# The order of weight loads, statistics and splits beside the experts' blocks of a routed layer, and which experts run in f32

## The chip, the cores and the metric

One Trainium2 chip, one core. The metric is the device time of one execution, in microseconds; of several runs the median is given.

## What is computed

```python
def reference(q, k, v, ...):
    x = attention(q, k, v)                  # causal by blocks of 64; 4 x 8 heads, 576 tokens, 64 wide
    x = x.transpose(0, 2, 1, 3).reshape(2304, 512)
    h = x @ w_in                            # 512 -> 2048
    x = elu(h) @ w_out                      # 2048 -> 512
    do = x @ w_skip > 0                     # about half of the tokens go on
    e = argmax(x[do] @ w_gate); gate = softmax's largest
    out = x.copy()
    for each expert i of 8:                 # w1[i] 512 x 1024, w2[i] 1024 x 512
        m = do & (e == i)
        out[m] += gate[m] * (relu(x[m] @ w1[i]) @ w2[i])
    return out
```

All inputs and the output are f32. With these inputs 1216 tokens are routed: 176, 2, 5, 91, 283, 192, 453 and 14 to the experts 0 to 7.

## The kernel before, in words

Attention and the dense layer run in chunks of 256 tokens, the last two stages of a chunk beside the next one's first; each chunk's tokens are routed as soon as it is through. After the last routing the experts follow. Expert 0's first 128 tokens and expert 2's (64 places) are known earlier and run beside the last routing. Then come **sections**: expert 6, 4, 5 (`ORDER`; 2 has nothing left), and a last section that holds the first block of each expert in `LAST`, 0, 3, 1 and 7. A section's first block is issued by `first_tokens`, further blocks of 128 tokens by `more_tokens` inside branches on the expert's count. First blocks of the experts in `SMALL` have 64 tokens. So with these inputs section 6 has four blocks of 128, section 4 has 64, 128 and 128 tokens, section 5 has 64 and 128, and the last one 64 tokens for 0, 1 and 7 and 128 for expert 3.

Tokens of a block are gathered by GpSimd (`gp`), transposed by SyncE's DMA (`mxt`, `mxwo`), multiplied with `w1` on TensorE (`hp`), made `r` and `hh` by ScalarE (`relu`) and VectorE, multiplied with `w2` (`y`), scaled by ScalarE into `o` and added to the output by GpSimd. In the last section experts of `PLAIN`, 1 and 7, are multiplied in f32, where one product is compiled into two instructions of TensorE; all others with f16 halves, three products for one.

For f16 the weights have to be prepared. An expert's weights are eight pages of 512 KB: half 0 is `w1` (four pages), half 1 is `w2`. A half is **loaded** by SyncE (`load_w`, L1447 and L1450), then come **statistics** of each page (`stat_w`, ScalarE L1465 into `jk` or VectorE L1467), a **scale** (`scale_w`: small steps on VectorE and one matmul `ns`, as TensorE sums over partitions) and **splits** of each page into high and low halves (`split_p`, ScalarE L1495 and VectorE L1496). A page needs a place in a list `FREE`, which is that of a page split before; the transfer waits until it is read.

What is prepared beside which block is written in the string `PREP`: section, colon, then a part per block between bars. `l` is a load, `s` the statistics, `c` the scale, `p` the splits; `c4-1` is expert 4, half 1. `split_beside` records these steps, `tokens` the block's. `Recorder.order` puts all steps of a part in an order by estimated costs, steps of the block (`urgent`) ahead and others where they fit in before the next urgent step of the engine; `rc.ready` keeps a step from being placed before a time within the part. Engines then run their lists in this order. What ends a section is a branch; the first matmul of the next section waits for ScalarE to have passed it.

`GATHERS` lists which tokens' gathers are issued within which section; `place_of` gives the tile.

Of the kernel before, what the change touches and what calls it, by code (L numbers as in the profile page):

```python
# [24 lines left out]
PLAIN = 1, 7  # L25
# [322 lines left out]
def tile_kernel(ctx, tc, q, k, v, w_in, w_out, w_skip, w_gate, w1, w2, out):  # L348
    nc = tc.nc
# [1119 lines left out]
    def scale_w(e, which):  # L1469
        acc = nrm[e][:, which]  # L1470
        cb = sm.tile([128, 1], BF16, tag="cb", bufs=2, name="cb")
        two = which and mixed(e)
        rc.vector.tensor_reduce(out=acc[:, 4:5], in_=acc[:, 2 * two:4], axis=AX.X, op=ALU.max if which else ALU.add)
        if two:
            rc.vector.scalar_tensor_tensor(out=acc[:, 4:5], in0=acc[:, 4:5], scalar=acc[:, 4:5], in1=acc[:, 0:1], op0=ALU.mult, op1=ALU.add)
            rc.vector.tensor_tensor(out=acc[:, 4:5], in0=acc[:, 4:5], in1=acc[:, 1:2], op=ALU.add)
        elif which:
            rc.vector.tensor_tensor(out=acc[:, 4:5], in0=acc[:, 4:5], in1=acc[:, 4:5], op=ALU.mult)
        rc.vector.tensor_copy(cb, acc[:, 4:5])
        p2 = misc([128, 1], "ns", "pv")  # L1480
        rc.tensor.matmul(out=p2, lhsT=ones16, rhs=cb, start=True, stop=True)
        rc.vector.tensor_copy(acc[:, 5:6], p2)
        scale_bits(acc[:, 5:6], acc[:, 6:7], acc[:, 7:8])
# [15 lines left out]
    def prep_steps(e, which):  # L1499
        P_ = functools.partial  # L1500
        return ([("stat", P_(stat_w, e, which, x)) for x in range(4)] + [("scale", P_(scale_w, e, which))]
                + [("split", P_(split_p, e, 4 * which + x)) for x in range(4)])
# [7 lines left out]
    def load_half(e, which, at=0.0):  # L1510
        for x in range(4):
            load_w(8 * e + 4 * which + x, at)
# [77 lines left out]
    def fac_w(e):  # L1590

        f = sm.tile([128, 1], F32, tag="fac", bufs=2, name="fac")
        fs = lst[:, e, :, 1]
        if e in PLAIN:
            return fs
        hs = half[:, e, C0[e], 1:2]
        nc.vector.tensor_tensor(out=f, in0=nrm[e][:, 0, 7:8], in1=nrm[e][:, 1, 7:8], op=ALU.mult)
        nc.vector.tensor_scalar(out=fs, in0=fs, scalar1=f, scalar2=2.0 ** 20, op0=ALU.mult, op1=ALU.mult)
        if e in SMALL:
            nc.vector.tensor_scalar(out=hs, in0=hs, scalar1=f, scalar2=2.0 ** 20, op0=ALU.mult, op1=ALU.mult)  # L1600
        return fs
# [80 lines left out]
    LAST = [0, 3, 1, 7]  # L1682
# [13 lines left out]
    def pre_gather(e):  # L1696
# [3 lines left out]
    GATHERS = {6: [(6, 2), (5, 0), (5, 1)], 4: [(4, 2), (0, 0), (3, 0)], 5: [(5, 2), (1, 0), (7, 0)]}  # L1700

    PREP = {int(e): [x.split() for x in h.split("|")] for e, h in (y.split(":") for y in (
        "6:l5-1 l3-0 c4-1 p4-1 s5-0|s5-1 c5-0 p5-0|c5-1 p5-1,4:l3-1 l1-0 s3-0|c3-0 p3-0 s3-1,5:l1-1 l7-0 c3-1 p3-1,7:l7-1").split(","))}
# [4 lines left out]
    def split_beside(e, part, at=5.0):  # L1708
        for h in sum(aside_of(e, part), []):
            if h[0] == "l":  # L1710
                load_half(int(h[1]), int(h[3]), at)
                continue
            for kind, f in prep_steps(int(h[1]), int(h[3])):
                if kind[1] == {"s": "t", "c": "c", "p": "p"}[h[0]]:
# [3 lines left out]
                    if h[0] == "s":  # L1718
                        rc.ready[len(rc.steps) - 1] = 2.0
# [10 lines left out]
    def first_tokens(e, fs):  # L1730
# [3 lines left out]
        rc.urgent = True  # L1734
        tokens(e, 0, place_of(e, 0), fs)
# [6 lines left out]
    def last_tokens(fs):  # L1742
# [3 lines left out]
        split_beside(LAST[-1], 0, 0.0)  # L1746
        rc.urgent = True
        for i, e in enumerate(LAST):
            tokens(e, 0, place_of(e, 0), fs[e], i)
# [124 lines left out]
    for h in "s4-0 s4-1 c4-0 p4-0 l5-0".split():  # L1874
# [8 lines left out]
    pre_gather(ORDER[2])  # L1883
# [6 lines left out]
    with tc.manual_schedule():  # L1890
# [10 lines left out]
        fs = {e: fac_w(e) for e in LAST}  # L1901
        tc.mark_branch_hint_location("last", cnt["last"] > 128, engines=[mybir.EngineType.PE])
        last_tokens(fs)
# [23 lines left out]
```

## Time and profile before

| | |
|---|---|
| median of 3 runs | 784.36 us (783.33 to 787.3) |
| the profiled execution | 785.88 us, its span 784.0 us |
| busy in the span | TensorE 700.9 us (89%), VectorE 570.4 (73%), ScalarE 511.3 (65%), GpSimd 92.0 (12%) |
| mean clock granted to TensorE | 0.952 of full speed |
| last routing ends, experts begin | 619.55 us |
| section 6 | 619.55 to 675.14 |
| section 4 | 675.14 to 715.21 |
| section 5 | 715.21 to 734.12 |
| last section | 734.12 to 773.79 |
| end | 784.0 |

Times of the sections are from the start of the span; each begins with TensorE's first matmul of it. The share of busy time is an average over stages with different limits, so that what a stage waits for has to be looked up in the stage. In the profile, PE is TensorE, PEld its loads of weights, ACT is ScalarE, DVE VectorE, POOL GpSimd, SP SyncE; a q behind a name is the queue of that engine. Buffer numbers are left out in names: pages of weights stand there as `p`, `pb`, `pc` and `pd`.

### The profile page before, as it was taken

What the parts mean: (1) busy time and instruction counts of PE and PEld (TensorE: products, weight loads), DVE (VectorE), ACT (ScalarE), POOL (GpSimd) and SP (SyncE); (2) the same over time, 40 slices, a digit from 0 to 9 for tenths busy, and PEclk for the clock granted to TensorE, in tenths of its full rate; (3) what the DMA queues carried; (4) which work ended last, traced back from release to release, by engine and by line L of the source; (5) the groups of instructions that cost most, each with busy time, mean ns of one, the idle gap of its engine ahead of it and who ended that gap; (6) DMA issues with size and microseconds to landing.
All of it is one profiled execution on the core that took longest, in us unless ns stands there. A gap on an engine that the chain in (4) does not pass through costs nothing. (4 is left out here: it accounts for less than half of the span.)

```text
span 784.0 us, 18160 instructions
## 1 busy us (share of the span) xinstructions
PE 700.9 (89%) x6766; PEld 466.2 (59%) x6766; DVE 570.4 (73%) x1710; ACT 511.3 (65%) x1132; POOL 92.0 (12%) x182
## 2 busy tenths in 40 slices
PE   4689997999998999989999999999999779869894
PEld 2467534764465655556656667675766656637673
DVE  5987999788997987978689648997777637143200
ACT  5966558989986886877587537673666667544310
POOL 2000000110001100101000100101040431313211
PEclk8579999999999999999999999999999898979998
DMA  9999899886979899999186189271546794492960
GB/s 263 298 257 281 258 255 199 168 134 125 183 146 139 146 197 180 157 184 179 38 145 125 32 173 382 74 224 42 182 106 185 151 269 109 80 273 46 292 158 5
DMA packets 279742, 134.03 MB, mean 171 GB/s; under 512 B 249291, under 2 KB 258005, under 8 KB 279120
## 3 DMA queue, kind: packets, MB, share of 16 engines
q1 hardware_dynamic: 275520, 125.42, 70.4%
q0 software_dynamic: 4112, 7.23, 4.6%
q8 instruction: 58, 0.95, 0.5%
q14 instruction: 52, 0.43, 0.2%
HBM read 74.12 MB, written 12.75 MB: 111 GB/s over the span
## 5 line engine op out<-in xcount | busy, mean ns | idle before, releaser
L310 PE MATMUL h<-xt,win 128*128 128x256 f16 x1344 | 158.1, 273 | 1.0 <-DVE n L310 1.0
L310 PE MATMUL y<-wout,g 128*128 128x512 f16 x672 | 157.4, 382 | 0.2 <-DVE g L310 0.2
L310 PEld LDWEIGHTS <-win 128*128 128x128 f16 x1344 | 127.6, 98 | 25.4 <-issue 3.1
L310 PEld LDWEIGHTS <-g 128*128 128x128 f16 x672 | 62.7, 98 | 70.8 <-issue 4.5
L310 ACT ACTIVATE ehl<-e,su 128x64 f16<-128x64 f32 (+4 forms) x208 | 85.7, 470 | 17.6 <-DMA et<-ehl 5.5
L310 ACT ACTIVATE e<-s,mx 128x64 f32<-128x64 f32 (+7 forms) x160 | 78.4, 493 | 25.3 <-DVE mx L310 10.5
L310 DVE SCALAR_TENSOR_TENSOR ehl<-e,su,ehl 128x64 f16<-128x64 f32 (+4 forms) x208 | 84.8, 441 | 6.9 <-ACT ehl L310 6.7
L310 DVE TENSOR_REDUCE mx<-s 128x1 f32<-128x64 f32 (+7 forms) x160 | 70.6, 449 | 13.5 <-PE s L310 12.8
L310 PE MATMUL s<-kt,qt 128*64 128x512 f16 (+7 forms) x640 | 62.8, 305 | 8.4 <-ACT e L310 5.5
L310 PE MATMUL xps<-et,vt 128*64 128x128 f16 (+1 forms) x1440 | 50.4, 219 | 16.2 <-DMA et<-ehl 9.9
L310 PEld LDWEIGHTS <-vt 128*64 128x64 f16 x1440 | 42.0, 115 | 35.5 <-issue 20.1
L310 PE MATMUL h<-xt,twi 128*128 128x256 f32 x256 | 62.1, 394 | 1.1 <-DVE g L310 1.1
L310 PE MATMUL y<-two,g 128*128 128x512 f32 x128 | 61.1, 610 | 0.0
L310 POOL MEMSET ehl<- 128x128 f16 x80 | 16.6, 213 | 357.4 <-DMA et<-ehl 275.6
L310 ACT ACTIVATE el<-h,col 128x512 f32<-128x512 f32 x56 | 38.2, 683 | 29.4 <-PE h L310 28.8
L310 PEld LDWEIGHTS h<-xt,twi 128*128 128x128 f32 x256 | 48.2, 195 | 10.9 <-DVE g L310 1.9
L310 PEld LDWEIGHTS <-qt 128*64 128x64 f16 x640 | 28.1, 114 | 43.2 <-issue 33.7
L310 PE MATMUL y<-p,hh 128*128 128x512 f16 (+1 forms) x222 | 41.0, 359 | 13.1 <-ACT hh L310 11.3
L310 ACT ACTIVATE g<-el,col 128x512 f16<-128x512 f32 x56 | 40.2, 717 | 18.9 <-DVE el L310 17.9
L310 PEld LDWEIGHTS <-hh 128*128 128x128 f16 (+1 forms) x336 | 26.4, 106 | 41.7 <-ACT hh L310 14.3
L1496 DVE SCALAR_TENSOR_TENSOR p<-p,n,p 128x1024 f16<-128x1024 f32 x30 | 38.3, 1281 | 12.3 <-ACT p L1495 12.2
L310 DVE TENSOR_TENSOR hh<-r,hh 128x256 f16<-128x256 f32 x38 | 15.9, 423 | 41.0 <-ACT hh L310 41.0
(231 smaller groups left out, 1185.5 us busy)
## 6 DMA issues: line engine op xcount, KB each, us to landing
p<-in_moe_w_dram SPq DMA_DIRECT2D x46, 512.0 KB, 7.1
rw<-in_moe_w_in_dram SPq DMA_DIRECT2D x16, 512.0 KB, 6.7
rw<-in_moe_w_out_dram SPq DMA_DIRECT2D x16, 512.0 KB, 5.0
pb<-in_moe_w_dram SPq DMA_DIRECT2D x13, 512.0 KB, 3.6
vflat<-in_v_dram SPq DMA_DIRECT2D x4, 1152.0 KB, 7.3
out_dram<-pay SPq DMA_DIRECT2D x18, 256.0 KB, 2.5
pay_d<-pay SPq DMA_DIRECT2D x18, 256.0 KB, 2.9
raw<-in_k_dram SPq DMA_DIRECT2D x16, 256.0 KB
```

The source lines that it names most:

```text
L310: rec.call(e, time, lambda: getattr(self.real, op)(*args, **kw), reads, writes, dma)
L1496: rc.call("dve", 1.2, lambda: nc.vector.scalar_tensor_tensor(out=half(1), in0=raw.t, scalar=sc, in1=half(0), op0=ALU.mult, op1=ALU.subtrac ...
```

## The change

`PLAIN` is expert 3 in place of 1 and 7. Expert 3 is the fourth largest, with 91 tokens and a block of 128; its splits go, and those of 1 and 7 come. `LAST` is 0, 1, 3, 7. Loads written `l` are recorded ahead of the block and urgent, so that they are the first of SyncE in the section; `m` is a load not placed before 5 us. Statistics are not placed before 4 us of a part in place of 2, scales not before 3, and `PREP` is rewritten so that most statistics are of pages loaded a section before. Scale and splits of expert 4's half 0 move from before the last routing into section 6, with its gathers, and `GATHERS` of the other sections change with that. The factors of the last experts (`fac_w`) are recorded within the last section.

```diff
--- before.py
+++ after.py
@@ -22,7 +22,7 @@
 
 GB = 8
 
-PLAIN = 1, 7
+PLAIN = 3,
 EARLY = 0, 2, 6
 
 SMALL = 0, 1, 4, 5, 7
@@ -1466,7 +1466,7 @@
         else:
             i = rc.call("dve", 1.14, lambda: nc.vector.tensor_reduce(out=a, in_=pl.t, axis=AX.X, op=ALU.max, apply_absolute_value=True), [pl.key], [a])
 
-    def scale_w(e, which):
+    def scale_w(e, which, wait=0.0):
         acc = nrm[e][:, which]
         cb = sm.tile([128, 1], BF16, tag="cb", bufs=2, name="cb")
         two = which and mixed(e)
@@ -1479,6 +1479,8 @@
         rc.vector.tensor_copy(cb, acc[:, 4:5])
         p2 = misc([128, 1], "ns", "pv")
         rc.tensor.matmul(out=p2, lhsT=ones16, rhs=cb, start=True, stop=True)
+        if wait:
+            rc.ready[len(rc.steps) - 1] = wait
         rc.vector.tensor_copy(acc[:, 5:6], p2)
         scale_bits(acc[:, 5:6], acc[:, 6:7], acc[:, 7:8])
 
@@ -1496,9 +1498,9 @@
         rc.call("dve", 1.2, lambda: nc.vector.scalar_tensor_tensor(out=half(1), in0=raw.t, scalar=sc, in1=half(0), op0=ALU.mult, op1=ALU.subtract),
                 [raw.key, sc, hl.key], [hl.key])
 
-    def prep_steps(e, which):
+    def prep_steps(e, which, wait=0.0):
         P_ = functools.partial
-        return ([("stat", P_(stat_w, e, which, x)) for x in range(4)] + [("scale", P_(scale_w, e, which))]
+        return ([("stat", P_(stat_w, e, which, x)) for x in range(4)] + [("scale", P_(scale_w, e, which, wait))]
                 + [("split", P_(split_p, e, 4 * which + x)) for x in range(4)])
 
     def prep(e, which):
@@ -1594,10 +1596,10 @@
         if e in PLAIN:
             return fs
         hs = half[:, e, C0[e], 1:2]
-        nc.vector.tensor_tensor(out=f, in0=nrm[e][:, 0, 7:8], in1=nrm[e][:, 1, 7:8], op=ALU.mult)
-        nc.vector.tensor_scalar(out=fs, in0=fs, scalar1=f, scalar2=2.0 ** 20, op0=ALU.mult, op1=ALU.mult)
+        rc.vector.tensor_tensor(out=f, in0=nrm[e][:, 0, 7:8], in1=nrm[e][:, 1, 7:8], op=ALU.mult)
+        rc.vector.tensor_scalar(out=fs, in0=fs, scalar1=f, scalar2=2.0 ** 20, op0=ALU.mult, op1=ALU.mult)
         if e in SMALL:
-            nc.vector.tensor_scalar(out=hs, in0=hs, scalar1=f, scalar2=2.0 ** 20, op0=ALU.mult, op1=ALU.mult)
+            rc.vector.tensor_scalar(out=hs, in0=hs, scalar1=f, scalar2=2.0 ** 20, op0=ALU.mult, op1=ALU.mult)
         return fs
 
     def block(e, xT, ts, fc, par, T=128):
@@ -1679,7 +1681,7 @@
 
 
     ORDER = [2, 6, 4, 5]
-    LAST = [0, 3, 1, 7]
+    LAST = [0, 1, 3, 7]
     XP = {2: 0, 6: 1, 4: 2, 5: 0}
 
     def place_of(e, j):
@@ -1697,26 +1699,33 @@
         for j in range(2):
             gather_to(e, j)
 
-    GATHERS = {6: [(6, 2), (5, 0), (5, 1)], 4: [(4, 2), (0, 0), (3, 0)], 5: [(5, 2), (1, 0), (7, 0)]}
+    GATHERS = {6: [(6, 2), (4, 0), (4, 1)], 4: [(4, 2), (5, 0), (5, 1), (0, 0), (1, 0)], 5: [(5, 2), (3, 0), (7, 0)]}
 
     PREP = {int(e): [x.split() for x in h.split("|")] for e, h in (y.split(":") for y in (
-        "6:l5-1 l3-0 c4-1 p4-1 s5-0|s5-1 c5-0 p5-0|c5-1 p5-1,4:l3-1 l1-0 s3-0|c3-0 p3-0 s3-1,5:l1-1 l7-0 c3-1 p3-1,7:l7-1").split(","))}
+        "6:l5-1 m1-0 c4-0 p4-0|c4-1 p4-1 s5-0|s5-1 c5-0 p5-0|c5-1 p5-1,4:l1-1 m7-0 s1-0|c1-0 p1-0 s1-1|c1-1 p1-1 s7-0,"
+        "5:l7-1 m3-0 c7-0 p7-0|s7-1,8:l3-1 c7-1 p7-1").split(","))}
 
     def aside_of(e, part):
         return PREP.get(e, [])[part:part + 1]
 
-    def split_beside(e, part, at=5.0):
+    def load_beside(e, part):
         for h in sum(aside_of(e, part), []):
             if h[0] == "l":
-                load_half(int(h[1]), int(h[3]), at)
+                load_half(int(h[1]), int(h[3]))
+
+    def split_beside(e, part):
+        for h in sum(aside_of(e, part), []):
+            if h[0] == "m":
+                load_half(int(h[1]), int(h[3]), 5.0)
+            if h[0] in "lm":
                 continue
-            for kind, f in prep_steps(int(h[1]), int(h[3])):
+            for kind, f in prep_steps(int(h[1]), int(h[3]), 3.0):
                 if kind[1] == {"s": "t", "c": "c", "p": "p"}[h[0]]:
                     rc.atom()
                     rc.shift = -150000 if kind == "scale" else 0
                     f()
                     if h[0] == "s":
-                        rc.ready[len(rc.steps) - 1] = 2.0
+                        rc.ready[len(rc.steps) - 1] = 4.0
                     rc.shift = 0
 
     def tokens(e, j, xT, fs, par=None):
@@ -1732,6 +1741,7 @@
         rc.begin()
         rc.late = rc.left
         rc.urgent = True
+        load_beside(e, 0)
         tokens(e, 0, place_of(e, 0), fs)
         rc.urgent = False
         for g in GATHERS[e]:
@@ -1739,12 +1749,14 @@
         split_beside(e, 0)
         rc.issue()
 
-    def last_tokens(fs):
+    def last_tokens():
 
         rc.begin()
         rc.late = rc.left
-        split_beside(LAST[-1], 0, 0.0)
+        load_beside(8, 0)
+        split_beside(8, 0)
         rc.urgent = True
+        fs = {e: fac_w(e) for e in LAST}
         for i, e in enumerate(LAST):
             tokens(e, 0, place_of(e, 0), fs[e], i)
         rc.urgent = False
@@ -1871,7 +1883,7 @@
     rc.atom()
     rc.urgent = False
     FREE += [Place(None, mo.tile([128, 1024], F32, tag="pay", bufs=2, name=f"pc{x}")) for x in (1, 2)]
-    for h in "s4-0 s4-1 c4-0 p4-0 l5-0".split():
+    for h in "s4-0 s4-1 l5-0".split():
         if h[0] == "l":
             load_half(int(h[1]), int(h[3]))
         else:
@@ -1880,7 +1892,6 @@
                     rc.shift = -50000 if kind == "scale" else 0
                     f()
             rc.shift = 0
-    pre_gather(ORDER[2])
     with tc.manual_schedule():
         rc.issue()
     left.clear()
@@ -1898,9 +1909,8 @@
             more_tokens(e, 0 if e == 2 else 1, fs)
             ng[0] = n0
             FREE.extend(WHL.pop(8 * e + x) for x in range(8))
-        fs = {e: fac_w(e) for e in LAST}
         tc.mark_branch_hint_location("last", cnt["last"] > 128, engines=[mybir.EngineType.PE])
-        last_tokens(fs)
+        last_tokens()
 
 
 _INS = ['q', 'k', 'v', 'moe_w_in', 'moe_w_out', 'moe2_w_skip', 'moe2_w_gate', 'moe2_w1', 'moe2_w2']
```

What it does to the order of instructions is shown at three places.

ScalarE at the end of section 6, the fourth block. In the names `pb`, `pc`, `pd` and `p` with a number are places of pages, `n` holds the scales, `o` is the scaled output. Before:

```order
L310 ACTIVATE r_10849<-hp 128x256
L310 ACTIVATE hh<-r_10849 128x256
L310 ACTIVATE r_10852<-hp 128x256
L310 ACTIVATE hh<-r_10852 128x256
L310 ACTIVATE o_1510<-y_10841,lists 128x512
L1767 COMPARE_AND_BRANCH
```

and now:

```order
L310 ACTIVATE r_10822<-hp 128x256
L310 ACTIVATE hh<-r_10822 128x256
L310 ACTIVATE r_10825<-hp 128x256
L310 ACTIVATE hh<-r_10825 128x256
L1497 ACTIVATE pd_1497<-pc_1531,n_90 128x1024
L1497 ACTIVATE pd_1498<-pc_1532,n_90 128x1024
L310 ACTIVATE o_1510<-y_10814,lists 128x512
L1497 ACTIVATE pc_1531<-p_1475,n_90 128x1024
L1497 ACTIVATE pc_1532<-p_7511,n_90 128x1024
L1779 COMPARE_AND_BRANCH
```

The block's `o` stood last; now two splits of expert 5's `w2` stand ahead of it and two behind it, ahead of the branch.

ScalarE in the third block of section 4, the last that is taken there. Before:

```order
L310 ACTIVATE r_11639<-hp 128x256
L310 ACTIVATE hh<-r_11639 128x256
L310 ACTIVATE r_11642<-hp 128x256
L310 ACTIVATE hh<-r_11642 128x256
L310 ACTIVATE o_1510<-y_11631,lists 128x512
L1767 COMPARE_AND_BRANCH
```

and now:

```order
L310 ACTIVATE r_11705<-hp 128x256
L1465 ACTIVATE jk,n_92<-p_7520 128x1024
L310 ACTIVATE hh<-r_11705 128x256
L1465 ACTIVATE jk,n_92<-p_7521 128x1024
L1497 ACTIVATE p_7514<-p_1475,n_86 128x1024
L1497 ACTIVATE p_7515<-p_7511,n_86 128x1024
L310 ACTIVATE o_1510<-y_11694,lists 128x512
L1465 ACTIVATE jk,n_92<-p_7522 128x1024
L1497 ACTIVATE p_1475<-p_7526,n_86 128x1024
L1497 ACTIVATE p_7511<-p_7518,n_86 128x1024
L1779 COMPARE_AND_BRANCH
```

Before, the block had nothing beside it; now statistics of expert 7 and splits of expert 1 are there, three of them behind `o`.

SyncE at the start of section 4; `in_moe_w_dram` stands for the weights, L1447 loads `w1`, L1450 `w2`. Before:

```order
L310 DMA_TRANSPOSE mxwo_1509<-gp_1505 128x8x128
L310 DMA_TRANSPOSE mxt_1507<-gp_1506 128x8x128
L310 DMA_TRANSPOSE mxt_1507<-gp_1505 128x8x128
L1450 DMA p_1475<-in_moe_w_dram 128x2x512
L1450 DMA p_7513<-in_moe_w_dram 128x2x512
L1450 DMA p_7528<-in_moe_w_dram 128x2x512
L1450 DMA p_7520<-in_moe_w_dram 128x2x512
L1447 DMA p_7521<-in_moe_w_dram 128x1024
L1447 DMA p_7522<-in_moe_w_dram 128x1024
```

and now:

```order
L1450 DMA p_1475<-in_moe_w_dram 128x2x512
L1450 DMA p_7511<-in_moe_w_dram 128x2x512
L1450 DMA p_7526<-in_moe_w_dram 128x2x512
L1450 DMA p_7518<-in_moe_w_dram 128x2x512
L310 DMA_TRANSPOSE mxwo_1509<-gp_1506 128x8x128
L310 DMA_TRANSPOSE mxt_1445<-gp_1505 128x8x128 x2
L1447 DMA p_7519<-in_moe_w_dram 128x1024
L1447 DMA p_7520<-in_moe_w_dram 128x1024
L1447 DMA p_7521<-in_moe_w_dram 128x1024
L1447 DMA p_7522<-in_moe_w_dram 128x1024
```

Four loads (`l1-1`) now come first, and the first of them go into the places `p_1475` and `p_7511`, the sources of the two splits at the end of section 6; the other four (`m7-0`) still stand behind three transposes.

## Rows read from the trace of the kernel before

**Rows 1.** Windows: start:end, length, PE PEld DVE ACT POOL busy (instructions), clock, DMA, GB/s.

```profile
619.55:675.14 55.59, 48.31 (x483) 33.71 (x483) 28.70 (x60) 33.25 (x60) 10.35 (x8) 0.88 0.63 157
675.14:715.21 40.07, 30.37 (x385) 21.02 (x386) 12.77 (x27) 19.66 (x39) 8.91 (x7) 0.87 0.67 173
715.21:734.12 18.91, 17.02 (x265) 13.13 (x266) 9.12 (x23) 9.61 (x18) 7.91 (x6) 1.00 0.67 134
734.12:773.79 39.67, 38.34 (x456) 31.98 (x456) 3.23 (x8) 7.96 (x19) 6.37 (x4) 1.00 0.59 175
```

**Rows 2.** TensorE's timeline, 616 to 697: start, length, instruction, [idle before, releaser].

```profile
619.55 1.79 PE L310 MATMUL hp<-mxt,p 128*128 128x128 f16 x24 [2.98 <-ACTq L1767]
622.48 0.16 PE L310 MATMUL ns<-cb,ones 128*128 128x1 bf16 x1 [1.14 <-DVE cb L310]
...
643.39 1.76 PE L310 MATMUL y<-p,hh 128*128 128x512 f16 x6 [2.79 <-ACT hh L310]
646.49 1.03 PE L310 MATMUL y<-p,hh 128*128 128x512 f16 x2 [1.34 <-ACT hh L310]
...
663.54 5.52 PE L310 MATMUL hp<-mxwo,p 128*128 128x128 f16 x96
...
696.53 1.03 PE L310 MATMUL y<-p,hh 128*128 128x512 f16 x2 [7.14 <-ACT hh L310]
```

**Rows 3.** ScalarE's timeline, 616 to 784.

```profile
617.28 2.17 ACT L1495 ACTIVATE pd<-pb,n 128x1024 f16<-128x1024 f32 x2
...
674.28 0.69 ACT L310 ACTIVATE o<-y,lists 128x512 f32<-128x512 f32 x1 [4.35 <-PE y L310]
...
693.72 1.06 ACT L1465 ACTIVATE jk<-p 128x1024 bf16<-128x1024 f32 x1 [8.62 <-DMA p<-in_moe_w_dram]
```

**Rows 4.** SyncE's queue in the timeline, 630 to 700.

```profile
684.39 4.31 SPq L310 DMA_TRANSPOSE mxt<-gp  x2
688.80 2.15 SPq L1450 DMA_DIRECT2D p<-in_moe_w_dram  x4
```

**Rows 5.** Windows of TensorE alone: start:end, length, busy (instructions), clock, DMA, GB/s.

```profile
622.00:626.00 4.00, 3.52 (x35) 0.50 0.80 85
...
645.00:650.00 5.00, 3.41 (x9) 0.50 1.04 410
...
676.00:678.00 2.00, 2.00 (x72) 1.00 0.34 37
...
696.00:702.00 6.00, 5.15 (x12) 0.50 1.03 403
```

**Rows 6.** Lines by shape, ScalarE, 616 to 784: count, busy us, mean ns, idle before.

```profile
L310 ACT ACTIVATE r<-hp 128x256 f32<-128x256 f32 x42 | 15.8, 379 | 33.9 <-PE hp L310 30.2 <-DVE pd L1496 2.0 <-remote 0.7
L310 ACT ACTIVATE hh<-r 128x256 f16<-128x256 f32 x38 | 15.5, 412 | 0.7
L1465 ACT ACTIVATE jk<-p 128x1024 bf16<-128x1024 f32 x7 | 7.4, 1050 | 8.7 <-DMA p<-in_moe_w_dram 8.6
L1495 ACT ACTIVATE p<-p,n 128x1024 f16<-128x1024 f32 x6 | 6.9, 1144 | 0.3 <-DVE pb L1496 0.3
```

**Rows 7.** TensorE's timeline, 697 to 784.

```profile
715.21 0.33 PE L310 MATMUL hp<-mxt,pb 128*128 128x64 f16 x6 [0.89 <-ACTq L1767]
...
721.17 0.51 PE L310 MATMUL hp<-mxt,pb 128*128 128x128 f16 x6
...
741.63 1.25 PE L310 MATMUL y<-p,hh 128*64 128x256 f16 x19 [1.30 <-issue]
...
752.02 7.25 PE L310 MATMUL hp<-x,p 128*128 128x64 f32 x64
...
762.81 0.66 PE L310 MATMUL hp<-x,pd 128*128 128x64 f32 x4
```

**Rows 8.** The page's costliest groups of the whole span: the dense layer's f32 products.

```profile
L310 PE MATMUL h<-xt,twi 128*128 128x256 f32 x256 | 62.1, 394 | 1.1 <-DVE g L310 1.1
L310 PE MATMUL y<-two,g 128*128 128x512 f32 x128 | 61.1, 610 | 0.0
```

## The prediction

> **What bounds the kernel now.** I read the profile from coarse to fine. The page gives TensorE 89% of the span, an average over stages with different limits. The change touches only the expert sections, so the second view is a table of windows, one for each of them [rows 1]: TensorE works 48.3 of 55.6 us in section 6 at a mean clock of 0.88, 30.4 of 40.1 us in section 4 at 0.87, 17.0 of 18.9 us in section 5 and 38.3 of 39.7 us in the last one, both at 1.00. So the first two lose time to waits and to the clock, and the last only to its own work. The third view, TensorE's timeline, names the waits [rows 2]: 2.98 us ahead of section 6 for ScalarE's queue, 1.14 for a scale, 2.79 and 1.34 us in its third block and 7.14 us in section 4, all three for ScalarE's `hh`. The fourth view says what ScalarE did there [rows 3]: ahead of section 6 it ran two page splits until 619.45, and TensorE began 0.1 us later; at 693.72 it began a statistic that had stood 8.62 us for a page of weights, with the block's `hh` queued behind. SyncE's queue tells why the page was late [rows 4]: the loads of section 4 stand behind two transposes, which ended at 688.70, so they were issued from 688.80, 13.7 us after the section began.
>
> Last I read the clock stretch by stretch [rows 5]: behind the waits of 2.98, 2.79 and 7.14 us TensorE had 0.50, which is 1.2 GHz, for 4, 5 and 6 us in these rows; behind the 0.9 us at section 4's start (`o` at 674.28, section from 675.14) it kept 1.00, 2.4 GHz. 35 `hp` filled those 4 us, and at 1.00 96 of them take 5.52 [rows 2], so they needed 2.0 and lost 2.0; the 5.15 busy us of the 6 lost half, 2.6. The edges, where the clock changes, add some tenths. I take 2.7 us for one such fall, between 2.4 and 3.2.
>
> **The change part by part.**
>
> *Ahead of the last routing.* Expert 4's first four splits move into section 6's first block. The two that ScalarE ran until 619.45 go, so section 6 begins after the routing's own last work and not after them. I take 616.7, as TensorE had ended the routing's work at 616.57 (619.55 less 2.98) [rows 2] and the two splits began at 617.28: **gain 2.85**. Expert 5's first load and expert 4's gathers change place as well; the load comes earlier into places already free, the gathers are needed a section later. I cost both at nothing; the cover is the 47 us of section 6, and if it failed the transposes of section 4's first block would come late, as in the second rival.
>
> *Section 6* (expert 6, four blocks of 128 tokens). An f16 block is worth 10.74 us, from its first `hp` at 663.54 [rows 2] to its `o` at 674.28 [rows 3]; four are 43.0. The waits of 2.79 and 1.34 us go, as the statistics that held up `hh` now are of pages loaded first in the section or one section earlier; with them two falls of the clock go, as nothing before them stands for 3 us. The scale matmul now waits to be ready; its next wait is in the third block, where I keep 1.0 for the 1.14 of before. New is the end: TensorE's first matmul of a section waits until ScalarE has passed the section's end, and in place of `o` alone (0.9 us) two splits stand behind `o`, 2.17 us the pair [rows 3], so 3.07. Sum 43.0+1.0+3.1 = 47.1 against 55.6: **gain 8.5**.
>
> *Section 4* (64, 128 and 128 tokens). A 64-token f16 block is 715.21 to 721.17, 5.96 us [rows 7]; with two of 128, 27.4. The 7.14 us go: SyncE issues the four pages of `l1-1` ahead of the transposes, which are for blocks 17 us or more away, and the statistics in this block are of pages loaded a section before. I leave 0.8 inside for `o` and `hh` behind statistics. At the end one statistic and two splits stand behind `o`: 0.9+1.05+2.17 [rows 3, 6], 4.1, with the semaphores 4.3. The fall of the clock behind 7.14 us is replaced by one behind the 3.07 us at this section's start, 2.7. Sum 27.4+0.8+4.3+2.7 = 35.2 against 40.1: **gain 4.9**.
>
> *Section 5* (64 and 128). Its work stays, 18.9; ahead of it stands the 4.3 us just counted, so the clock falls here too: **loss 2.7**.
>
> *Last section.* Before: expert 0, then 3, both split, 734.12 to 752.02, then 1 in 10.79 and 7 in 10.98 us to 773.79 [rows 1, 7], with 1.30 us for issue. Now 0, 1 and 7 cost 5.96 each. The 128-token f32 block is not in the trace. First product: 64 matmul instructions; at 64 tokens they take 7.25 us [rows 7], which is the least; twice that, 14.5, is the most, if time goes with columns at this rate. But the f32 `h` of the dense layer has 256 columns at 243 ns (62.1 us by 256) [rows 8], so 128 columns are near 122 ns, 7.8 us; I take 7.4, as this row is nearest. Second product: 16 of 512 columns at 477 ns (61.1 by 128) [rows 8], 7.6 us; or twice the 3.54 us that lie between 759.26 and 762.81 for two half-width outputs side by side, 7.1. I take 7.2, so the block is 14.6 (14.35 to 22). Sum 17.9+14.6+1.3 = 33.8 against 39.7: **gain 5.9**.
>
> One rule speaks against giving f32 up for 1 and 7 and to 3. By the Trainium skill, FP8 and Floating Point Precision, TensorE Precision Notes, "True FP32: 4 passes through PE array"; a split product here is three. By that ratio a 64-token f32 block would be 8.0 us, the change would gain some 4 us on the two small experts and lose 3.6 on expert 3, and the total would be 770.5. The rows give 10.8 to 11.0 for 64 tokens, so at this size the rule does not hold here, while for 128 tokens it gives 14.3, near my 14.6. The sum stays with the rows.
>
> *More of the preparation.* One expert more is split: eight splits and eight statistics, mostly in ScalarE's and VectorE's queues beside blocks. By [rows 6] ScalarE has in section 6 16 `r`, 16 `hh`, 4 `o`, 16 splits, 6 statistics: 40.0 of 47.1 us; in section 4 10, 10, 3, 8 and 10: 29.6 of 32.5. It is covered by TensorE's time and by little; that is the fourth rival.
>
> The tail behind TensorE's end, 10.2 us, stays. **Sum**: 2.85+8.5+4.9-2.7+5.9 = 19.4. Against the profiled execution, 785.88 (span 784.0), that is 766.5; this one stands 1.5 above the median of the runs, 784.36, from which I get **765.0**.
>
> **The rivals.**
>
> 1. *The clock does not fall at the two joins.* The waits of 3.1 and 4.3 us are near the 2.79 that was followed by 0.50, which speaks against; for it, a wait may come out shorter if ScalarE takes a split between `hh`s. Then 2 x 2.7 less: 759.6. Chance 0.15.
>
> 2. *The change does not do what it says: the loads stay late.* SyncE's first two pages of section 4 go into places that expert 5's last two splits read, at the very end of section 6, and all of the queue stands behind them. If a wait like 7.14 us stays in section 4, whose fall of the clock then comes on top of or in place of the one at its start, 7 to 9 us come back: 773. Against: the statistics of this section's first block are of other pages. Chance 0.12.
>
> 3. *It cancels*: the f32 block at its upper bound (7.4 more) together with the second rival, about 781 or above, counts as no change. Chance 0.05.
>
> 4. *Slower: ScalarE becomes the bound.* Every block whose last `hh` waits behind splits costs 3.07 us and a fall of 2.7, together 5.8. There are six joins inside the sections (three, two, one). From the fourth on that is over the gain: four make 23.2 and 788.2. For it, the 40.0 of 47.1 and 29.6 of 32.5 us; against it, ScalarE's list has the splits mostly after the block's last `hh`, and inside a section TensorE does not wait for ScalarE's queue to end. Chance 0.03.
>
> **How the numbers follow.** The forecast, 765.0, has 0.65: its bounds are the clock fall (2.4 to 3.2, twice: 1), the f32 block (0.3 less to 7.4 more), waits inside (2 either way). Of it 0.02 is what I leave to the four-pass rule of the Trainium skill's page above, with 770.5. The range goes to 756 below, past the first rival with its tolerance, and to 775 above, past the second; outside lie 0.2. Less than 0.5%, 3.9 us, can't be told from no change here. Faster: all but the last two rivals, 0.92; same 0.05; slower 0.03.
>
> **What would show it.** Section 6 should begin near 616.7 less what earlier stages drift, and last 47 us with one wait of about 3 us at its end and none over 1.5 inside; section 4 should start at 0.50, show no wait for a page of weights over 2 us and last 35; section 5 21.6; the last 34, with `hp` of expert 3 at 113 to 122 ns and 5.96 us for each of 0, 1 and 7. I am wrong if ScalarE waits for weights in section 4, if `hp` f32 at 128 tokens takes over 130 ns, or if TensorE waits 3 us inside a section.

## The result, and the profile after

| | before | changed |
|---|---|---|
| median, first comparison | 785.36 us (783.33 to 787.3) | 761.2 us (759.11 to 767.84) |
| ratio, 95% interval | | 0.9707 (0.9642 to 0.9773) |
| median, second comparison (run e8), later | 785.44 us (781.09 to 787.69) | 770.25 us (767.43 to 772.76) |
| ratio, 95% interval | | 0.9803 (0.9773 to 0.9834) |
| profiled execution, its span | 785.88, 784.0 us | 760.7, 758.8 us |

The kernel is faster by 2 to 3%; 765.0 had been forecast. Both intervals lie clear of 1; a gain of 2% or more is sure by the first alone, as the second reaches 0.9834. That the two comparisons lie 9 us apart for one kernel is part of the result, and the second one is taken up below. Medians here and below are of all runs, ratios and intervals of the fast ones alone, and one run of e10 (770.23 us) is slow. First the windows by section of the changed kernel, columns as in [rows 1]:

```profile
614.10:661.29 47.19, 42.74 (x484) 30.99 (x485) 30.75 (x63) 36.69 (x64) 13.29 (x9) 1.00 0.66 159
661.29:693.30 32.01, 27.20 (x386) 20.78 (x386) 18.27 (x38) 27.63 (x51) 12.74 (x9) 1.00 1.05 251
693.30:712.49 19.19, 18.26 (x265) 14.40 (x265) 12.51 (x27) 11.47 (x22) 6.34 (x5) 0.91 0.92 245
712.49:748.39 35.90, 33.47 (x513) 28.12 (x513) 9.83 (x25) 11.84 (x23) 7.17 (x4) 0.95 0.50 131
```

Section 6 fell from 55.59 to 47.19 us, section 4 from 40.07 to 32.01, section 5 stayed (18.91 and 19.19), the last one fell from 39.67 to 35.90. With the earlier start, 614.10 in place of 619.55, these are the 25 us between the two spans; the tail stayed (10.21 and 10.41). ScalarE is now busy in 27.63 of section 4's 32.01 us.

TensorE's timeline, the rows that answer to [rows 2, 7]:

```profile
614.10 2.23 PE L310 MATMUL hp<-mxt,p 128*128 128x128 f16 x37 [0.64 <-PEq L1779]
617.69 2.11 PE L310 MATMUL hp<-mxt,p 128*128 128x128 f16 x35 [1.36 <-issue]
...
661.29 0.42 PE L310 MATMUL hp<-mxwo,p 128*128 128x64 f16 x9 [2.89 <-ACTq L1779]
...
665.08 3.05 PE L310 MATMUL y<-pb,hh 128*64 128x256 f16 x48 [0.83 <-ACT hh L310]
```

```profile
693.30 0.42 PE L310 MATMUL hp<-mxt,pb 128*128 128x64 f16 x9 [3.93 <-ACTq L1779]
...
712.49 0.60 PE L310 MATMUL hp<-mxt,p 128*128 128x64 f16 x15 [0.89 <-ACTq L1779]
714.41 5.45 PE L310 MATMUL hp<-mxt,p 128*128 128x64 f16 x128 [1.32 <-issue]
720.92 0.20 PE L310 MATMUL hp<-mxt,p 128*128 128x64 f16 x1 [1.06 <-issue]
...
728.84 0.39 PE L310 MATMUL hp<-x,p 128*128 128x128 f32 x2
729.06 0.83 PE L310 MATMUL hp<-x,pb 128*128 128x128 f32 x6
729.73 0.39 PE L310 MATMUL hp<-x,p 128*128 128x128 f32 x2
...
735.82 3.60 PE L310 MATMUL y<-p,r 128*128 128x512 f32 x8
739.26 3.60 PE L310 MATMUL y<-pb,r 128*128 128x512 f32 x8
742.69 0.34 PE L310 MATMUL hp<-mxwo,pb 128*128 128x64 f16 x6
```

None of the three waits for `hh` that [rows 2] showed inside the sections is left; the longest is 0.83. The waits of 2.89 and 3.93 at the joins, where one section ends and the next begins, are new, and so is one of 1.36 us, behind the 37th matmul of section 6, that has no releaser in the profile ("issue"). What had stood behind the 2.79 in section 6 before is not in the rows above: a statistic that waited for a page of expert 5's second half. SyncE's queue and ScalarE, before:

```profile
636.05 1.05 SPq L1450 DMA_DIRECT2D pb<-in_moe_w_dram  x2
```

```profile
641.88 1.06 ACT L1465 ACTIVATE jk<-pb 128x1024 bf16<-128x1024 f32 x1 [5.65 <-DMA pb<-in_moe_w_dram]
```

Those pages were issued 16.5 us into section 6; the changed kernel issues the same half 0.9 us ahead of its start, and no statistic of it waits for a page. Why the weights were no longer late stands in SyncE's queue and on ScalarE:

```profile
613.24 0.97 SPq L1450 DMA_DIRECT2D pc<-in_moe_w_dram  x2
...
662.82 3.00 SPq L1450 DMA_DIRECT2D p<-in_moe_w_dram  x4
668.17 1.36 SPq L310 DMA_TRANSPOSE mxwo<-gp  x1
```

```profile
659.02 2.17 ACT L1497 ACTIVATE pc<-p,n 128x1024 f16<-128x1024 f32 x2
...
672.58 1.05 ACT L1465 ACTIVATE jk<-p 128x1024 bf16<-128x1024 f32 x1
...
691.03 2.17 ACT L1497 ACTIVATE p<-p,n 128x1024 f16<-128x1024 f32 x2
```

The four pages of section 4 were issued from 662.82, 1.5 us behind the start of section 4 (13.7 before [rows 1, 4]), ahead of the transposes; the statistic of the first, at 672.58, waited for nothing, where the one of [rows 3] had waited 8.62 us. 659.02 and 691.03 are the two splits behind `o` at the joins. The clock, as in [rows 5]:

```profile
662.00:663.00 1.00, 1.00 (x41) 1.00 0.55 98
...
696.00:697.00 1.00, 1.00 (x24) 0.50 0.51 111
...
716.00:717.00 1.00, 1.00 (x24) 0.50 1.00 361
```

Behind 2.89 us it stayed at 1.00 here, behind 3.93 it fell to 0.50 (1.2 GHz), and so it did in the last section, where 0.89 and 1.32 us of waiting follow each other.

### The profile page after: what moved, and what is told of

It is laid out like the page before. It is cut to its first block, busy times and chain, and to the rows that moved or that the text cites. A ratio compares the mean times of both kernels' runs of the same rounds, so it can differ in the third digit from the quotient of the medians.

```text
span 758.8 us, 18338 instructions
## 1 busy us (share of the span) xinstructions
PE 687.6 (91%) x6824; PEld 460.3 (61%) x6824; DVE 584.1 (77%) x1737; ACT 524.6 (69%) x1152; POOL 95.5 (13%) x182
## 5 line engine op out<-in xcount | busy, mean ns | idle before, releaser
L310 ACT ACTIVATE el<-h,col 128x512 f32<-128x512 f32 x56 | 38.2, 683 | 30.2 <-PE h L310 29.6
L1498 DVE SCALAR_TENSOR_TENSOR p<-p,n,p 128x1024 f16<-128x1024 f32 x35 | 44.4, 1279 | 6.4 <-ACT p L1497 6.4
L310 PEld LDWEIGHTS <-p 128*128 128x128 f16 x840 | 42.5, 100 | 11.2 <-issue 6.7
L310 DVE SCALAR_TENSOR_TENSOR g<-el,col,g 128x512 f16<-128x512 f32 x56 | 41.7, 744 | 3.7 <-ACT g L310 3.6
```

The lines of the kernel that those rows point to most:

```text
L310: rec.call(e, time, lambda: getattr(self.real, op)(*args, **kw), reads, writes, dma)
L1498: rc.call("dve", 1.2, lambda: nc.vector.scalar_tensor_tensor(out=half(1), in0=raw.t, scalar=sc, in1=half(0), op0=ALU.mult, op1=ALU.subtrac ...
```

## The experiments

The theory: loads first take the waits for weights away, and that is most of the gain; the exchange of f32 and the moved splits give a few us each; what remains are waits for ScalarE's list at the joins. The main rival: the exchange, or the statistics a section later, is what pays. All sections, from each kernel's profiled execution (start of section 6, then lengths, us):

| kernel | median, ratio | 6 begins | 6 | 4 | 5 | last | span |
|---|---|---|---|---|---|---|---|
| before | 785.36 | 619.55 | 55.6 | 40.1 | 18.9 | 39.7 | 784.0 |
| changed | 761.2, 0.9707 | 614.10 | 47.2 | 32.0 | 19.2 | 35.9 | 758.8 |
| e1 f32 back | 763.47, 0.9762 | 611.83 | 49.4 | 31.7 | 17.3 | 37.9 | 758.8 |
| e2 loads late | 778.94, 0.9935 | 613.36 | 49.6 | 41.1 | 22.7 | 42.6 | 780.6 |
| e3 splits ahead | 764.41, 0.9767 | 619.10 | 45.6 | 33.6 | 19.2 | 34.6 | 762.4 |
| e4 two copies more | 768.03, 0.9787 | 617.54 | 51.8 | 34.1 | 19.2 | 34.3 | 767.3 |
| e5 loads first alone | 770.02, 0.9789 | 621.53 | 46.3 | 31.1 | 21.8 | 39.5 | 771.1 |
| e6 statistics of 7 later | 766.62, 0.9755 | 614.39 | 47.2 | 35.1 | 20.5 | 36.5 | 764.0 |
| e7 and less on ScalarE | 764.57, 0.9734 | 617.77 | 46.2 | 30.9 | 21.5 | 35.6 | 762.2 |
| e8 changed again | 770.25, 0.9803 | 618.62 | 48.0 | 36.4 | 20.3 | 37.0 | 771.0 |
| e9 f32 second | 768.97, 0.9788 | 612.71 | 47.2 | 37.8 | 21.7 | 37.0 | 766.8 |
| e10 e7 and e9 | 765.74, 0.9718 | 618.45 | 47.4 | 32.5 | 20.5 | 34.8 | 764.0 |

The 95% intervals of the ratios reach 0.3 to 0.7% to each side; only those of the changed kernel's first comparison and of e10 lie beyond 2% as a whole, and only e2's lies within it. e1 to e4 ran on one chip, e5 to e7 on another, e8 to e10 on a third, each group beside the kernel before (783.79, 784.28 and 785.44 us). As one kernel's two medians differ by 9 us, whole times are best compared within a group. Sections are of one execution each, so that they can stand off from the median: e2's is the slowest of its ten (782.36), e8's the slowest of its six (772.76). Sections end where the next one's first matmul begins, the last one with TensorE's last matmul.

### Loads first: e2 and e5

e2 takes them out of the changed kernel:

```diff
-        load_beside(e, 0)
         tokens(e, 0, place_of(e, 0), fs)
...
-            if h[0] == "m":
-                load_half(int(h[1]), int(h[3]), 5.0)
             if h[0] in "lm":
+                load_half(int(h[1]), int(h[3]), 0.0 if e == 8 else 5.0)
                 continue
```

(`load_beside(8, 0)` of the last section goes too.)

> The loads recorded behind the block and not before 5 us, as in the kernel before; all else as changed. If loads first are what took away the waits for weights: expert 1's second half is issued behind two transposes at about 676 in place of 663, its first statistic in section 4's second block waits about 6 us with hh behind it, and the clock falls: section 4 38 to 41 us in place of 32.0, section 6 47 to 49, in all 767 to 772. If it is the statistics a section later that did it: within 2 us of the changed kernel.

778.94 us, ratio 0.9935 (0.99 to 0.997), above the 767 to 772 expected: by the ratios two thirds (of the second comparison's gain) to just under four fifths (of the first's) are gone. On the same chip e1 and e3, with loads first, took 763.47 and 764.41, so that late loads cost about 15 us there. SyncE, ScalarE and TensorE of e2 in section 4:

```profile
671.07 5.79 SPq L310 DMA_TRANSPOSE mxt<-gp  x2
676.96 1.56 SPq L1450 DMA_DIRECT2D p<-in_moe_w_dram  x3
```

```profile
681.67 1.06 ACT L1465 ACTIVATE jk<-p 128x1024 bf16<-128x1024 f32 x1 [5.77 <-DMA p<-in_moe_w_dram]
...
693.70 1.06 ACT L1465 ACTIVATE jk<-p 128x1024 bf16<-128x1024 f32 x1 [2.47 <-DMA p<-in_moe_w_dram]
...
721.06 1.06 ACT L1465 ACTIVATE jk<-p 128x1024 bf16<-128x1024 f32 x1 [4.12 <-DMA p<-in_moe_w_dram]
```

```profile
683.19 4.50 PE L310 MATMUL y<-pb,hh 128*128 128x512 f16 x12 [3.75 <-ACT hh L310]
...
723.11 2.79 PE L310 MATMUL y<-pc,hh 128*128 128x512 f16 x12 [3.28 <-ACT hh L310]
```

The transposes hold SyncE until 676.86, the loads follow; the first statistic waits 5.77 us for its page, `hh` stands behind it, TensorE waits 3.75 us; then a second of 2.47. The price I had for section 4 (41.1 measured, 38 to 41 expected) was at its upper end. What I had not counted is that it goes on: a statistic of section 5 waits 4.12 us for the page of the next load and TensorE 3.28, and the last section is 6.7 us longer than the changed kernel's, with 6.5 us of waits without a releaser. Statistics a section later, with the exchange and the moved splits, are worth 5 us without the loads, then: an expert's second half is still loaded and counted in one section.

e5 puts the same thing alone into the kernel before (shown for the list; `load_beside` and `split_beside` are those of the change):

```diff
-        "6:l5-1 l3-0 c4-1 p4-1 s5-0|s5-1 c5-0 p5-0|c5-1 p5-1,4:l3-1 l1-0 s3-0|c3-0 p3-0 s3-1,5:l1-1 l7-0 c3-1 p3-1,7:l7-1"
+        "6:l5-1 m3-0 c4-1 p4-1 s5-0|s5-1 c5-0 p5-0|c5-1 p5-1,4:l3-1 m1-0 s3-0|c3-0 p3-0 s3-1,5:l1-1 m7-0 c3-1 p3-1,7:l7-1"
```

> The kernel before with nothing but the place of the loads changed: the half that is needed first is issued first in its section, the other one stays at 5 us; f32 for 1 and 7, the splits ahead of the last routing and the rest of the list as before. If loads first carry most of the change by themselves: the waits of 2.79, 1.34 and 7.14 us and the falls of the clock behind them go, section 6 about 49 us (55.6 before), section 4 about 30.5 (40.1 before), in all 766 to 770. If they only serve together with statistics a section later: 778 or more.

770.02 us, ratio 0.9789 (0.972 to 0.9857), as the theory had it: 14 us (784.28 to 770.02) by the place of the loads alone. Section 6 came out 2.7 us below what was expected, section 4 at 31.1. TensorE of e5:

```profile
621.53 2.72 PE L310 MATMUL hp<-mxt,p 128*128 128x128 f16 x24 [2.98 <-ACTq L1775]
...
636.35 0.16 PE L310 MATMUL ns<-cb,ones 128*128 128x1 bf16 x1 [1.14 <-DVE cb L310]
...
667.82 0.25 PE L310 MATMUL hp<-mxwo,pb 128*128 128x64 f16 x3 [0.98 <-ACTq L1775]
...
673.48 1.74 PE L310 MATMUL y<-pb,hh 128*64 128x256 f16 x24 [1.27 <-ACT hh L310]
...
698.91 0.34 PE L310 MATMUL hp<-mxt,pb 128*128 128x64 f16 x6 [0.89 <-ACTq L1775]
...
712.65 2.69 PE L310 MATMUL y<-p,hh 128*128 128x512 f16 x6 [2.25 <-ACT hh L310]
```

The 2.98 ahead of section 6 and the 1.14 for a scale stand as in [rows 2], the waits of 2.79, 1.34 and 7.14 don't. 0.98 and 0.89 at the joins: with one expert less to prepare nothing stands behind `o`. One wait of 2.25 is new in section 5; ScalarE had splits ahead of that `hh` and waited for no page, and behind it the clock fell.

### The exchange of f32: e1

```diff
-PLAIN = 3,
+PLAIN = 1, 7
...
-    LAST = [0, 1, 3, 7]
+    LAST = [0, 3, 1, 7]
...
-    4:l1-1 m7-0 s1-0|c1-0 p1-0 s1-1|c1-1 p1-1 s7-0, 5:l7-1 m3-0 c7-0 p7-0|s7-1, 8:l3-1 c7-1 p7-1
+    4:l3-1 m1-0 s3-0|c3-0 p3-0 s3-1|c3-1 p3-1, 5:l1-1 m7-0, 8:l7-1
```

(in section 6 `m1-0` becomes `m3-0`; the gathers of 1 and 3 change places)

> Expert 1 and 7 in f32 again and 3 split, the new order of loads kept, so one expert less is prepared. If the exchange is worth what the blocks cost: the last section is 6.0+10.7+10.8+11.0+1.3 = 39.7 us in place of 35.9, but section 4's third block has no statistics of expert 7, so its wait before section 5 falls from 3.9 to about 3 and the clock may not fall behind it (1.7): the total about 762, 760 to 765, near the changed kernel. If the exchange were the main gain of the change, 775 or more.

763.47 us; by the whole time this can't be told from the changed kernel. The rival, that the exchange is the main gain, falls. By sections it is what was expected in kind: the last is 37.9 in place of 35.9 (39.7 expected), section 5 is 17.3 in place of 19.2. TensorE of e1 at the start of sections 5 and last:

```profile
692.92 0.42 PE L310 MATMUL hp<-mxt,pb 128*128 128x64 f16 x9 [2.30 <-ACTq L1779]
...
710.26 4.30 PE L310 MATMUL hp<-mxt,p 128*128 128x64 f16 x120 [0.99 <-ACTq L1779]
```

2.30 in place of 3.93 ahead of section 5, and no fall of the clock behind it. So what the last section gains by the exchange, the preparation of one expert more costs before it. (By the counts of tokens expert 3, with 91, is the fifth largest and not the fourth; the blocks are as said.)

### The splits ahead of the routing: e3

```diff
-    for h in "s4-0 s4-1 l5-0".split():
+    for h in "s4-0 s4-1 c4-0 p4-0 l5-0".split():
...
-    6:l5-1 m1-0 c4-0 p4-0|...
+    6:l5-1 m1-0|...
```

> Scale and splits of expert 4's first half ahead of the last routing again; the gathers stay where the change put them. If that work stood in the path there: section 6 begins 5.4 us later, near 619.5, behind a wait of about 3 us, and the clock falls behind it (2.4), with nothing back in section 6, as two splits stand behind o there still: 766 to 769. If the work was only moved: section 6 is shorter by as much, within 1.5 us of the changed kernel.

764.41 us, between the two. Its TensorE rows:

```profile
619.10 5.52 PE L310 MATMUL hp<-mxt,p 128*128 128x128 f16 x96 [2.83 <-ACTq L1779]
...
664.74 0.25 PE L310 MATMUL hp<-mxwo,pb 128*128 128x64 f16 x3 [2.89 <-ACTq L1779]
```

The wait of 2.83 is back ahead of section 6, which begins at 619.10. But section 6 is the shortest of all, 45.6, as behind that wait there is none without a releaser, and the clock did not fall. In every kernel whose section 6 begins without the wait (all but before, e3 and e5) one of 0.60 to 2.35 us stands behind the same 37th matmul, and in e1, e2 and e4 the clock fell behind it. Counted from a point ahead, the start of the last 22 `y` of the dense layer, section 6 begins 3.7 us earlier in the changed kernel than in e3 (26.2 and 29.9; 27.3 in e8), and by the lengths in the table 0.6 to 4 us are given back in it. What the move is worth lies between a small loss and 3 us, not at 5.4.

### The joins: e4, e6, e7

e4, behind the fourth block of section 6:

```diff
                 rc.issue()
+                if e == 6 and j == 3:
+                    for _ in range(2):
+                        nc.scalar.activation(out=junk.t, in_=WHL[48].t.bitcast(F16)[:, 0:1024], func=AF.Copy)
```

> Two more ScalarE copies of 128x1024, whose result is not used, behind the o of section 6's fourth block. If ScalarE's list sets the start of section 4: the wait of 2.89 us becomes about 5.0, and the clock falls to 0.50 behind it for 3 to 6 us as it did behind 3.93: 2.1 plus 1.6 to 2.7, total about 764.7. If the clock stays at 1.00 as behind 2.89: 762.8. If the start of section 4 hangs on something else, no change.

```profile
669.36 0.64 PE L310 MATMUL hp<-mxwo,p 128*128 128x64 f16 x9 [4.93 <-ACTq L1779]
```

4.93 us, 2.04 more for two copies, and section 4 is 2.1 longer than the changed kernel's, where the clock had not fallen. So the join is ScalarE's list, instruction for instruction. The median, 768.03 (762.23 to 770.29), is above the expected 764.7; section 6 lost 2.35 us behind its 37th matmul (1.36 in the changed kernel) and a fall of the clock besides.

e6 takes work off ScalarE in section 4:

```diff
-    4:...|c1-1 p1-1 s7-0, 5:l7-1 m3-0 c7-0 p7-0|s7-1
+    4:...|c1-1 p1-1,      5:l7-1 m3-0 s7-0|c7-0 p7-0 s7-1
```

> The changed kernel with the statistics of expert 7's first half moved from section 4's third block to section 5's first, and its scale and splits to section 5's second. ScalarE has 27.6 of 32.0 us to do in section 4 and 11.5 of 19.2 in section 5. If ScalarE's list sets the join: one split in place of a statistic and two splits stands behind o, the wait ahead of section 5 is about 2.0 in place of 3.93 and the clock does not fall behind it: section 4 about 30, section 5 about 17.5, total 3 to 4 less than the changed kernel, 757. If the work only moves the wait to the end of section 5: no less than 760.

e7 is e6 with one line more:

```diff
-EARLY = 0, 2, 6
+EARLY = 0, 2, 6, 5
```

> As the run before it, and all four statistics of expert 5's second half on VectorE in place of two on ScalarE (the largest magnitude for all four pages in place of sums of squares for two). One split in place of two stands behind o at the end of section 6: its wait falls from 2.89 to about 1.9. 1 us less than the run before it, about 756. If VectorE is late instead, the wait appears inside section 6's third block, ahead of ns: no gain.

Both expectations failed as times: 766.62 and 764.57. The joins did what was said. TensorE of e7:

```profile
663.93 0.42 PE L310 MATMUL hp<-mxwo,p 128*128 128x64 f16 x9 [2.08 <-ACTq L1779]
...
694.78 0.42 PE L310 MATMUL hp<-mxt,pb 128*128 128x64 f16 x9 [2.44 <-ACTq L1779]
...
704.54 0.33 PE L310 MATMUL hp<-mxt,pb 128*128 128x128 f16 x3 [0.43 <-issue]
705.29 0.38 PE L310 MATMUL hp<-mxt,pb 128*128 128x128 f16 x4 [0.42 <-issue]
706.03 0.23 PE L310 MATMUL hp<-mxt,pb 128*128 128x128 f16 x1 [0.36 <-issue]
706.75 0.22 PE L310 MATMUL hp<-mxt,pb 128*128 128x128 f16 x1 [0.49 <-issue]
```

2.08 and 2.44 in place of 2.89 and 3.93, no fall of the clock behind either. But section 5 is 21.5: four waits of 0.36 to 0.49 without a releaser stand in its second block, and the clock fell there later. The kernel before had two such waits in the same block, the changed one, which came to it 3.93 us late, none. In e6, section 4 was 35.1, with 2.40 us for `hh` in its first block, where the changed kernel had 0.83 with the same instructions. Ahead of that `hh` ScalarE's `r` had waited 3.31 us for what the profile calls "remote", which returns below. One execution of each does not decide this, so the next three were run side by side.

### The changed kernel again, and two orders: e8, e9, e10

> The changed kernel once more. The join of section 6 and 4 is 2.89 us in every look so far that has two splits there; the clock fell behind it in four of five kernels and not in the first look at the changed one. If that is chance from run to run: the fall of 1.6 to 2.7 us comes in this look, the second wait without a releaser in section 6 stands at the same 37th matmul (1.4 to 2.4 us), and the median is 761 to 765. If it is a trait of this kernel's own code: the clock stays at 1.00 behind 2.89 and the median is 759 to 762.

770.25 us, 9 above the first comparison, beside a kernel before that had not moved. Its section 4, on TensorE and ScalarE, and its clock:

```profile
666.64 0.64 PE L310 MATMUL hp<-mxwo,p 128*128 128x64 f16 x9 [2.90 <-ACTq L1779]
...
673.66 4.19 PE L310 MATMUL y<-pb,hh 128*64 128x256 f16 x48 [2.71 <-ACT hh L310]
```

```profile
672.92 0.38 ACT L310 ACTIVATE r<-hp 128x256 f32<-128x256 f32 x1 [3.09 <-remote]
```

```profile
667.64:668.64 1.00, 1.00 (x24) 0.50 0.52 96
...
674.64:675.64 1.00, 1.00 (x14) 0.50 0.89 262
```

The same join, 2.90, and here the clock fell; then `r` waited 3.09 us for "remote", `hh` with it, TensorE 2.71, and the clock fell once more. The same stands in e9 (3.04, TensorE 2.85), as in e6. That is section 4 at 36.4 in place of 32.0. Section 6 began 4.5 us later, 3.4 of it ahead of the last routing, in work that the change doesn't touch: the last 22 `y` of the dense layer began at 591.31 and not at 587.91. So between these two executions the same program differs in three things, the stages ahead, a wait that the profile calls remote and the falls of the clock; of none do these runs show the cause, nor what part the chip has in it.

e9 (`LAST = [0, 3, 1, 7]`, and the gathers of 1 and 3 exchanged) and e10 (e7 with the same):

> The changed kernel with the experts of the last section in the order 0, 3, 1, 7 in place of 0, 1, 3, 7 (and the two gathers that go with it exchanged), so that the f32 block, with 80 instructions in 14.5 us, stands behind one 64-token block and not behind two with 144 each. If the waits without a releaser there (1.3 and 1.1 us in the changed kernel, 2.7 to 6.5 in others, one fall of the clock with them) come from matmuls that run faster than their instructions arrive: no more than 1.3 us of them in this section and it lasts 33 to 34.5 us in place of 35.9. If they belong to the section's start whatever runs there: 35 to 37 as before.

> Both together: the order 0, 3, 1, 7, expert 7's first statistics in section 5 and all of expert 5's second half on VectorE. Waits ahead of sections 4 and 5 of 2.0 to 2.4, behind which the clock has not fallen in any look, in place of 2.89 and 3.93: 2 us of waits and 2 to 4 us of falls less, up to 2 us back as waits without a releaser in section 5. Against the changed kernel of the same chip 1 to 4 us less, 758 to 761. If what ScalarE no longer delays is delayed by missing instructions in full: no difference.

e9: 768.97, no different from e8. TensorE at the start of its last section:

```profile
719.44 0.60 PE L310 MATMUL hp<-mxt,p 128*128 128x64 f16 x15 [0.90 <-ACTq L1779]
723.30 3.95 PE L310 MATMUL hp<-mxt,p 128*128 128x64 f16 x81 [3.26 <-issue]
```

3.26 us, again behind the section's first 15 matmuls, and a section of 37.0 in place of the 33 to 34.5 that would have spoken for matmuls running faster than their instructions arrive. But that wait stands in the block of expert 0, which both orders have first, so the run neither shows that idea nor rules it out. e10: 765.74 us, ratio 0.9718 (0.9674 to 0.9762) against e8's 0.9803 (0.9773 to 0.9834) on the same chip; the two intervals do not meet. It is the best of the three there, by 4.5 us against e8 (1 to 4 expected) and 3.2 against e9, though above the 758 to 761 that I had. Its waits at the joins are 2.09 and 2.82; behind 2.09 the clock fell all the same, behind 2.82 it did not.

## Why the prediction was right, and where not

- **What bounds the sections, and the loads.** Right. The waits for `hh` of 2.79, 1.34 and 7.14 were gone, and e5 and e2 show that the place of the loads is what took them away, alone (14 us) and in the changed kernel (about 15 beside e1 and e3 of the same chip, 9 to 18 by which of its two medians one takes). The 2.79 and 1.34 stood in section 6's second block and not, as the prediction reads them, in its third; nothing hangs on that. The second rival, that the loads stay late, fell: they were issued 1.5 us into section 4. Its price, 7 to 9 us in section 4, is near what e2 measured there (9.1), but not the 10 more that e2 lost in sections 5 and last.
- **The start of section 6**, forecast 616.7, was 614.10, and 618.62 in e8, whose dense layer came 2.8 us later than before. The term took off the wait and left TensorE's own path as it was; but from the dense layer's last 22 `y` to the end of the routing's last matmuls (613.47 in place of 616.57) it took 25.6 us and 26.7 in e8, in place of 28.1 (27.1 in e3 and e5, where the splits stand ahead as well). What was missed the other way is the wait behind the 37th matmul, 1.36 here and 0.6 to 2.35 elsewhere, which stands only where the wait for ScalarE doesn't. e3 puts the whole between a small loss and 3 us.
- **Section 6**: 47.1 forecast, 47.19 and 48.02 measured, but with 0.19 for the scale in place of 1.0, 2.89 at the join in place of 3.07, and the 1.36 that I had not seen.
- **Section 4**: 35.2 forecast, 32.01 and 36.38 measured. The 0.8 inside was 0.83 (2.71 in e8), the join 3.93 and not 4.3. The step that failed in the first profile is the fall of the clock behind 2.89 us, 2.7 in the sum; it came in e8, as in e1, e2, e3, e6 and e9. Where it came it was over-sized too: with the same instructions and waits in section 4, but for the join ahead of it, e3 and e4 lasted 1.6 and 2.1 us longer than the changed kernel. So of the first rival, no fall at the joins, the first comparison shows half: none behind 2.89, one behind 3.93.
- **Section 5**: 21.6 forecast, 19.19 and 20.33 measured. The fall came, but cost 1.3 and not 2.7: the first block's 96 `hp` took 4.3 us in place of 3.0, and then the clock was back. The two waits without a releaser of the kernel before, 0.52 and 0.48, did not come.
- **Last section**: 33.8 forecast, 35.90 and 36.99 measured. The f32 block was right: the eight matmuls from one `hp` group to the next take 0.89 us, 111 ns each (113 at 64 tokens), `y` 6.87 us from 735.82 to 742.69; with that the third rival falls, which had it at its upper bound. (The prediction's 7.1 for `y` counts from 759.26, but the first `y` stands at 759.21, which makes 7.2.) Mis-sized is the term for `issue`: 1.3 was 2.4 (2.9 in e8), and a fall of the clock came with it.
- **The four-pass rule.** Expert 3's block took 14.0 us (64 times 111 ns and 6.87). By the Trainium skill, FP8 and Floating Point Precision, TensorE Precision Notes, "True FP32: 4 passes through PE array"; with three for a split product that gave the prediction's estimate of 14.3 us, so the trace agrees at 128 tokens. At 64 it does not: the same 64 instructions take as long for half the columns, and the block 10.8 to 11.0 us in place of the estimated 8.0.
- **Slower, by ScalarE as the bound**: fell; the 40.0 and 29.6 us of work counted for sections 6 and 4 were 36.69 of 47.19 and 27.63 of 32.01, and the waits of 3 to 4 us stayed at the two joins.

Against the profiled execution the sum said 766.5; the changed kernel's was 760.7 and e8's 772.76, for one program. In the first the start and sections 4 and 5 were 8.2 us shorter than forecast and the last 2.1 longer; in e8 all but section 5 were longer. The basis, which waits go and which come, was right, but that 765.0 lies between the two medians is in part luck: the terms missed by up to 3 us each, in both directions. That a term like the fall of the clock is paid in one execution and not in the next was not in it.

## What to carry to other kernels

Look at what stands ahead of a load in its queue before looking at its size: the same loads, issued first in their section (in section 4 12 to 14 us earlier), gave 14 us by themselves, and no other part of the change, taken by itself, can be told from nothing by the whole time. A wait taken from one engine shows what it had covered: where ScalarE no longer held TensorE, TensorE waited without a releaser for 0.6 to 2.4 us, so count on less than the wait. And where one kernel's medians differ by 9 us, read an edit in its section of the trace, and time it on one chip beside the kernel that it is compared with.

## What was not expected of the hardware

Behind waits of nearly one length the clock did not do the same each time. At the starts of sections, behind 2.82 to 2.98 us TensorE was soon at 0.50 in eight profiles (before and e5 ahead of section 6; e1, e2, e3, e6, e8 and e9 ahead of section 4) and stayed at 1.00 in three places (the changed kernel ahead of section 4, e3 ahead of section 6, e10 ahead of section 5). Behind 3.93 it fell each time (changed, e3, e4, e8, e9). Of the waits of 2.08 to 2.44 there (e1, e6, e7, e10) only e10's 2.09 was followed by a fall; but inside sections 2.25 (e5) and 2.40 (e6) were too. Of two waits of 2.99 without a releaser, in the last section, e2's was followed by a fall and e3's was not. So in these runs a wait's length alone does not tell. A 128-token f32 product took no longer than one of 64 tokens for `hp`: 111 and 113 ns for an instruction. The waits without a releaser stand at the same matmul from kernel to kernel, though their lengths differ (0.60 to 2.35 us behind the 37th); what they wait for, the profile doesn't show. In the last section they stand 128 matmuls apart, behind the 15th and the 143rd (changed, e2, e4, e8) or the 14th, 142nd and 270th (e6), and behind the 143rd or 142nd alone in e3 and e7. That would fit instructions that arrive in portions, but no run here tests it.
